# The opening of an attention and experts kernel, ordered anew for each engine

## The chip, the cores and the metric

The kernel runs on one core of a Trainium2 chip. The metric is the device time of one execution in microseconds (us); the median of several executions is what two kernels are compared by. Five engines work side by side, each through its own queue in order: TensorE (PE, with its weight loads as PEld), VectorE (DVE), ScalarE (ACT), GpSimd (POOL), and SyncE (SP), which here issues nearly all DMAs. TensorE's clock has two levels in the records, 2.4 GHz (granted clock 1.0) and 1.2 GHz (0.5).

## The reference, cut to what matters

```
scores = q @ k.T / 8, causal; a = softmax(scores); local = a @ v        # B=2, H=8, S=576, D=64
phi(x) = where(x > 0, x, exp(x) - 1) + 1
mem_out = (phi(q) @ M_prev) / (phi(q) . z_prev + 1e-6)
attn = g * mem_out + (1 - g) * local,  g = sigmoid(beta)                  # per head
x = attn as [1152 tokens, 512]
x = relu(x @ w_in)**2 @ w_out                                             # 512 -> 2048 -> 512
out = sum over 4 experts of p_e * (relu(x @ w1_e) @ w2_e)                 # 512 -> 1024 -> 512
```

## The kernel before, in words

The 1152 tokens are nine tiles of 128 (`TILES`), in three chunks: chunk 0 is tiles 7 and 8 (the first 128 positions of both batches), chunk 1 is tiles 0 to 3, chunk 2 is tiles 4 to 6. The first feed-forward layer, `ffn1`, runs once for each chunk; while it runs for one chunk, the attention of the next is woven in (`mix`), so TensorE always has matmuls of a feed-forward layer to put between those of attention. Only for chunk 0 is there no layer to hide behind: its attention is the **opening**, and TensorE's dense work begins with the first `hpa` matmul of `mm_in` (L101), which needs the finished tokens `first_x` (tile `y`, written at L222).

In the opening chunk 0 has four units: (tile 7, heads 0 to 3), (8, 0 to 3), (7, 4 to 7), (8, 4 to 7), which are called u0, u1, u2, u3 below. A unit goes through score matmuls (L303, into a bank of PSUM), four masked row maxima on VectorE (`top`, L189, and the bias `nb`, L314), four exps on ScalarE (L320), a transpose on TensorE (L332) copied back by VectorE (L335), and the value matmuls (L352). Beside it the feature maps `phi(q)` are made in two halves (exp L181, VectorE L183 and L184), `mem` multiplies them by the memory `mzd` in three groups of heads (L365, copied by ScalarE, L368), and `combine` scales and adds the two parts for each tile (`zeroth` L199 to L204, `first` L211 and L212, `second` L218 to L222).

The order of the opening is a string of step names, `order`, carried out step by step inside `tc.manual_schedule()`, where every engine keeps the written order. Outside that block only TensorE keeps the written order; for the other engines a planner with its own idea of durations decides, and it may put an instruction that it takes to be ready into an earlier gap of its engine, the opening's gaps too. `tc.keep_in_program_order(x)` forbids that for one instruction: x stays behind what was written before it on its engine.

Three more pieces of work meet here. `convert` (the steps `c` and `f`) turns the 64-bit weight words of `ffn1` into floats, one half block at a time: a DMA of 512 KB (L647), two ScalarE passes (L657, L660), two VectorE passes (L661, L664), and a write of 256 KB to DRAM (L667); there are 32 half blocks, the layer eats them in order, and four buffers hold words that are on their way. `value_scale` takes ten sums of squares of `v` on ScalarE (L405), wanted only in chunk 2. `c1` is the attention of chunk 1: its first two pairs of units are scored in the opening (`S0`, `S1`), the others, its feature maps and the squares are written later, in `rest`.

Of the kernel before, what the change touches and what calls it, by code (L numbers as in the profile page):

```python
# [10 lines left out]
F32 = mybir.dt.float32  # L11
# [5 lines left out]
AF = mybir.ActivationFunctionType  # L17
# [4 lines left out]
P = 128  # L22
# [30 lines left out]
def attention_then_experts(ctx, tc, qa, ka, va, qc, kc, vc, mz, beta, w1, probs, w2, out):  # L53
# [122 lines left out]
        nc.vector.tensor_scalar(out=gate1, in0=gate, scalar1=-1.0, scalar2=1.0, op0=ALU.mult, op1=ALU.add)  # L176
        yield

    def phi(out, e, q):

        nc.scalar.activation(out=e, in_=q, func=AF.Exp)  # L181
        yield
        nc.vector.tensor_scalar_min(e, e, 1.0)  # L183
        nc.vector.scalar_tensor_tensor(out=out, in0=q, scalar=1.0, in1=e, op0=ALU.add, op1=ALU.max)  # L184
        yield
# [7 lines left out]
    def combine(t, pool, xl, xm, sm, guard, pv, ps, eng, nm=1, gate1=gate1):  # L193


        cf = pool.tile([P, 2, H], F32, tag="cf", name="cf", bufs=2)

        def zeroth():
            nc.vector.tensor_scalar_add(cf[:, 0], sm, guard)  # L199
            nc.vector.tensor_scalar_add(cf[:, 1], xm[:, :, D], 1e-6)  # L200
            nc.vector.reciprocal(out=cf, in_=cf)
            nc.vector.tensor_mul(cf[:, 0], cf[:, 0], gate1)
            nc.vector.tensor_mul(cf[:, 1], cf[:, 1], gate)
            nc.gpsimd.tensor_mul(xm[:, :, 0:D], xm[:, :, 0:D], cf[:, 1, :, None].to_broadcast([P, H, D]))  # L204

        def first():
            if not pv:
                eng.tensor_mul(xl, xl, cf[:, 0, :, None].to_broadcast([P, H, D]))
            for hs, part in pv() if pv else ():
                n = hs.stop - hs.start  # L210
                nc.vector.tensor_mul(xl[:, hs], part, cf[:, 0, hs, None].to_broadcast([P, n, D]))  # L211
            eng.tensor_add(xl, xl, xm[:, :, 0:D])  # L212

        def second():
            tp = ps.tile([P, NK, P], F32, tag="m", name="tp", bufs=nm)
            xf = xl.rearrange("p h d -> p (h d)")
# [14 lines left out]

    def opening(c0, c1, first_layer):

        sc, ph, low, gt = [c0.scores(p) for p in c0.pairs], c0.phis(0), [], gates()
        later = [c1.scores(p) for p in c1.pairs[:2]]
        units = [u for p in c0.pairs for u in p]
        xs = []
        third = (slice(0, 3), slice(3, 6), slice(6, 8))
        steps = dict(
            g=lambda: next(gt), c=lambda: next(cv), f=lambda: next(cv), w=lambda: next(first_layer), l=lambda: c1.load(1),  # L240
            x=lambda: xs.extend(c0.combine(t) for t in range(*CHUNKS[0])),
            a0=lambda: xs[0][0](), a1=lambda: xs[0][1](), a2=lambda: low.append(xs[0][2]()), a3=lambda: low[0](),
            b0=lambda: xs[1][0](), b1=lambda: xs[1][1](), b2=lambda: low.append(xs[1][2]()), b3=lambda: low[1](),
        )
        for i in range(2):
            steps[f"s{i}"] = lambda i=i: next(sc[i])
            steps[f"v{i}"] = lambda i=i: [c0.values(u) for u in c0.pairs[i]]
            steps[f"S{i}"] = lambda i=i: next(later[i])
            steps[f"p{i}"] = lambda i=i: next(ph[i])
        for i in range(4):  # L250
            steps[f"t{i}"] = lambda i=i: c0.turn(units[i], nc.vector)
        for i in range(3):
            steps[f"m{i}"] = lambda i=i: c0.mem(0, third[i])
        order = (
            "s0 p0 g s0 g s0 s1 s0 p1 s0 s1 l f s1 t0 p0 x s1 t1 S0 s1 p1 m0 v0 t2 S0 m1 t3 "
            "m2 v1 S0 c S0 a0 b0 S1 S0 a1 S1 b1 c S1 a2 b2 w S1 c b3 a3 S1 c"
        )
        for k in order.split():
            steps[k]()

    def attention_a(c, pool, eng, banks):
# [9 lines left out]
        def load(r):  # L271
            raw = pool.tile([P, H, P], F32, tag="qa", name="qa", bufs=2)
            ka_t[r] = kva.tile([P, H, P], F32, name=f"ka{r}")
            for hs in (slice(0, 4), slice(4, 8)):
                nc.sync.dma_start(out=ka_t[r][:, hs], in_=ka[r, :, hs])
                nc.sync.dma_start(out=raw[:, hs], in_=qa[r, :, hs])
            q[r] = [raw, None, pool.tile([P, B, H, D + 1], F32, tag="xm", name="xm", bufs=2)]
            load_v(r)

        def load_v(r):  # L280
            for b in range(B):
# [2 lines left out]

        def phis(r):
            e = q[r][1] = pool.tile([P, H, P], F32, tag="phia", name="phia", bufs=2)
            return [phi(e[:, hs], e[:, hs], q[r][0][:, hs]) for hs in (slice(0, 4), slice(4, 8))]

        def s_(pair):
            scs = {}  # L290
            for u in pair:
# [3 lines left out]
                scs[u] = banks[0].tile([P, 512], F32, tag="s", name="sc", bufs=banks[1])  # L295
# [74 lines left out]
        def combine_(t):  # L370
# [13 lines left out]
            )  # L384

        return SimpleNamespace(
            pairs=pairs, load=load, phis=phis, scores=s_, turn=t_, values=v_, mem=mem, combine=combine_,
        )

    def value_scale(pool, banks):  # L390

        todo = [(b, k) for k in (3, 4) for b in range(B)]
        vsq = pool.tile([P, 3 * B + len(todo)], F32, tag="vsq", name="vsq", bufs=1)

        def stage(b, k):
            x = pool.tile([P, 4, P], F32, tag="vstage", name="vstage", bufs=2)
            nc.sync.dma_start(out=x, in_=vc[b, :, :, k].rearrange("j p d -> p j d"))
            return x.rearrange("p j d -> p (j d)")

        parts = [va_t[b, r].rearrange("p h d -> p (h d)") for r in range(3) for b in range(B)]  # L400
        for i in range(vsq.shape[1]):
            if i < len(todo):
                parts.append(stage(*todo[i]))
            sq = pool.tile([P, 512], BF16, tag="sq", name="sq", bufs=2)
            nc.scalar.activation(out=sq, in_=parts[i], func=AF.Square, accum_out=vsq[:, i:i + 1])  # L405
            yield
        total = banks[0].tile([P, vsq.shape[1]], F32, tag="m", name="total", bufs=banks[2])
        nc.tensor.matmul(total, lhsT=ones, rhs=vsq, start=True, stop=True)
        nc.vector.tensor_reduce(out=vs, in_=total, axis=AX.X, op=ALU.add)
        power(vs, vi, 77)  # L410
        nc.vector.tensor_mul(gate1v, gate1, vi[:, 0:1].to_broadcast([P, H]))
        yield

    def rest(x, scale):
# [7 lines left out]
        for i, pair in enumerate(x.pairs):  # L422
            t, kn, h0, nh = pair[0]
            r = TILES[t][0][1] // P
            if i >= 2:
                plan(i - 2, 0, lambda p=pair: run(x.scores(p)))
            for u in pair:
                plan(i, 2, lambda u=u: x.turn(u))
# [5 lines left out]
            if h0 + nh == H:  # L434
                for n, u in enumerate(pair):
# [4 lines left out]
                        parts[0]()  # L440

                    plan(i, 5 + n, make)
                    plan(i, 7 + n, lambda parts=parts: parts[1]())
# [8 lines left out]
    def attention_b(pool, ps):  # L452
# [158 lines left out]
        for i in range(len(units) + lag + 3):  # L611
# [9 lines left out]
            if 0 <= i - lag < len(units):  # L621
                t, j = units[i - lag]
                m = [values(t, j)[0]] + m
                if j == 3:
                    xl, xm, mx, nb, sm = st[t]
                    fs = combine(t, pool, xl, xm, sm, 1e-9 * 2.0**14, None, ps, nc.gpsimd, gate1=gate1v)
                    m = m + [lambda fs=fs: (fs[0](), fs[1]())]
# [10 lines left out]
    def convert(pool):  # L638
# [10 lines left out]
        for i in range(3):  # L649
            fetch(i)  # L650
        yield
        for i, (f, half) in enumerate(todo):
            fetch(i + 3)
# [94 lines left out]
    with ExitStack() as ca:  # L748
# [5 lines left out]
        with tc.tile_pool(name="ps_0", bufs=1, space=PSUM) as ps_0:  # L754
            with tc.manual_schedule():
# [372 lines left out]
```

## Time before, and what the profile says of it

| | before |
|---|---|
| median of 3 runs | 743.21 us (741.28 to 744.14) |
| the profiled execution | 740.5 us, of which the span from first to last instruction is 738.7 us |
| TensorE busy | 686.9 us, 93% of the span |
| VectorE, ScalarE, GpSimd busy | 549.1, 430.2, 241.4 us |
| TensorE busy from 36 us to 136 us | 90.4 of 100 us |
| first matmul of the feed-forward layer | 35.48 us after the span's start |

All instants are counted from the start of the span. Before 35.48 us TensorE has only the small matmuls of the opening; after it, it is busy nine tenths of the time or more to the end.

### The profile page before, as it was taken

The numbers are of one execution on the slowest core, as the hardware profiler recorded it, in microseconds if no ns is written. First come the engines' busy times: TensorE is split into PE (matmuls) and PEld (weight loads), VectorE is DVE, ScalarE is ACT, GpSimd is POOL, SyncE is SP. The second block draws the span as 40 slices with busy tenths as digits, with TensorE's granted clock in tenths as the row PEclk, the third lists the DMA queues.
The fourth block names the chain that finished last, engine by engine and source line by source line (L and its number), as shares of the span: only waits on it lengthen the run. The fifth ranks groups of instructions, "written<-read, shape, count | busy, mean of one in ns | idle before, by whom it ended". The sixth has DMA issues, their size and how long they took to land.

```text
span 738.7 us, 12576 instructions
## 1 busy us (share of the span) xinstructions
PE 686.9 (93%) x4604; PEld 487.1 (66%) x4604; DVE 549.1 (74%) x1057; ACT 430.2 (58%) x844; POOL 241.4 (33%) x249
## 2 busy tenths in 40 slices
PE   6588899989899998999999989999999999999997
PEld 4466777767677787989865655566655555555553
DVE  4867858479989874746879968989787685867763
ACT  5687767376665534887776756655535353535341
POOL 1101101253533237645623433344432323141400
PEclk7799999999999999999999999999999999999999
DMA  9788765177885543685412323233342222100002
GB/s 286 229 297 289 254 219 180 58 262 222 196 197 122 122 114 83 238 302 169 131 59 93 108 85 115 87 113 94 109 168 75 100 81 91 58 1 1 1 1 71
DMA packets 65422, 101.25 MB, mean 137 GB/s; under 512 B 32656, under 2 KB 34704, under 8 KB 65360
## 3 DMA queue, kind: packets, MB, share of 16 engines
q1 hardware_dynamic: 65216, 100.45, 44.5%
q8 instruction: 36, 0.59, 0.3%
q14 instruction: 26, 0.21, 0.1%
q10 hardware_dynamic: 144, 0.00, 0.0%
HBM read 82.87 MB, written 10.75 MB: 127 GB/s over the span
## 4 chain that ended last, share of the span: by engine, by line
PE 52%; DVE 18%; ACT 11%; DMA 9%; issue 6%; POOL 3%; SPq 0%; DVEq 0%; ACTq 0%; POOLq 0%
PE o L1016 19%; PE pe L924 16%; DMA raw<-in_w 4%; PE y L723 3%; PE hpb L106 3%; PE pv L584 2%; DMA wraw<-w1s 2%; DVE bits L661 2%; PE y L721 2%; POOL w L84 2%; PE hpa L101 2%; DVE g L713 1%; ACT a L320 1%; DVE a L189 1%; PE sc L516 1%
## 5 line engine op out<-in xcount | busy, mean ns | idle before, releaser
L1016 PE MATMUL o<-w,g 128*128 128x512 f16 x864 | 218.5, 379 | 7.0 <-DVE g L940 3.8
L924 PE MATMUL pe<-xs,wu 128*128 128x256 f16 (+1 forms) x1344 | 196.5, 286 | 2.1 <-DVE h L945 2.0
L924 PEld LDWEIGHTS <-wu 128*128 128x128 f16 x1344 | 131.0, 98 | 70.3 <-issue 3.8
L1016 PEld LDWEIGHTS <-g 128*128 128x128 f16 x864 | 83.7, 98 | 77.8 <-DVE g L940 7.1
L84 POOL TENSOR_TENSOR w<-wraw,w 128x512 fp32r<-128x512 f32 x49 | 73.1, 1498 | 104.6 <-ACT w L83 104.3
L939 ACT ACTIVATE g<-h 128x512 f16<-128x512 f32 (+1 forms) x64 | 43.3, 677 | 105.7 <-DVE h L945 105.7
L723 PE MATMUL y<-g,w 128*128 128x512 f32 (+1 forms) x384 | 90.7, 372 | 1.5 <-ACT w L83 0.7
L954 POOL TENSOR_TENSOR u<-u,p 128x256 f32<-128x256 f32 (+1 forms) x32 | 32.3, 1011 | 132.7 <-ACT p L953 110.9
L723 PEld LDWEIGHTS y<-g,w 128*128 128x128 f32 x384 | 68.2, 189 | 9.7 <-ACT w L83 1.0
L940 DVE SCALAR_TENSOR_TENSOR g<-h,g 128x512 f16<-128x512 f32 (+1 forms) x64 | 50.4, 788 | 26.3 <-ACT g L939 26.0
L106 PE MATMUL hpb<-x,w 128*128 128x512 f32 x192 | 53.2, 414 | 4.7 <-DVE r L707 4.6
L945 DVE SCALAR_TENSOR_TENSOR h<-pe,u 128x256 f32<-128x256 f32 (+1 forms) x96 | 42.8, 451 | 19.8 <-PE pe L924 15.7
L891 POOL TENSOR_TENSOR ws<-raw 128x256 f32<-128x256 f32 x32 | 23.3, 727 | 101.9 <-issue 88.7
L888 DVE SCALAR_TENSOR_TENSOR wu<-ws,wpow,wu 128x512 f16<-128x512 f32 x64 | 50.9, 835 | 2.9 <-ACT wu L899 2.9
L833 DVE SCALAR_TENSOR_TENSOR w<-raw,wpow,w 128x512 f16<-128x512 f32 x64 | 48.0, 755 | 0.7 <-ACT w L832 0.6
L83 ACT ACTIVATE w<-wraw 128x512 fp32r<-128x512 f32 x64 | 39.5, 623 | 13.0 <-DMA wraw<-w1s 6.6
L106 PEld LDWEIGHTS hpb<-x,w 128*128 128x128 f32 x192 | 36.3, 196 | 13.6 <-DVE r L707 6.4
L832 ACT ACTIVATE w<-raw,wpow 128x512 f16<-128x512 f32 x64 | 44.6, 709 | 0.9 <-PE o L1016 0.9
L829 ACT ACTIVATE junk<-raw 128x1024 bf16<-128x1024 f32 x32 | 33.5, 1048 | 19.0 <-DMA raw<-in_w 18.9
L189 DVE CUSTOM_DVE_ANT_0 a<-sc,mask 128x384 f32<-128x384 f32 (+4 forms) x80 | 35.9, 477 | 11.1 <-PE sc L303 5.5
L204 POOL TENSOR_TENSOR xm<-xm,cf 128x512 f32<-128x512 f32 x9 | 10.6, 1184 | 102.1 <-ACT at L337 42.7
L106 PE MATMUL hpc<-x,w 128*128 128x384 f32 x192 | 37.3, 339 | 3.1 <-POOL w L84 2.0
(159 smaller groups left out, 1200.0 us busy)
## 6 DMA issues: line engine op xcount, KB each, us to landing
raw<-in_w SPq DMA_DIRECT2D x64, 512.0 KB, 3.4
w<-in_w SPq DMA_DIRECT2D x32, 512.0 KB, 4.4
wraw<-w1s SPq DMA_DIRECT2D x64, 256.0 KB, 3.1
w1s<-bits SPq DMA_DIRECT2D x32, 256.0 KB, 2.5
kraw<-in_kc SPq DMA_DIRECT2D x8, 576.0 KB, 4.1
vraw<-in_vc SPq DMA_DIRECT2D x8, 320.0 KB, 3.7
qraw<-in_qc SPq DMA_DIRECT2D x4, 512.0 KB, 4.9
out<-acc SPq DMA_DIRECT2D x8, 256.0 KB, 2.1
```

The lines of the kernel that those rows point to most:

```text
L84: eng.tensor_sub(w[:, 1], raw, w[:, 0].bitcast(F32))
L106: nc.tensor.matmul(acc, lhsT=w[:, a, kk * P:(kk + 1) * P], rhs=xs_r[c][:, b, kk, :], start=(i == 0), stop=(i == 3 * NK - 1),)
L189: nc.vector.tensor_tensor_reduce(out=dst, in0=sc, in1=msk, op0=ALU.add, op1=ALU.max, scale=1.0, scalar=-3.0e38, accum_out=m)
L723: nc.tensor.matmul(yacc[d], lhsT=w[:, a, d * P:(d + 1) * P], rhs=g[:, b], start=(first and i == 0), stop=(last and i == 2),)
L832: nc.scalar.activation(out=w0, in_=x, func=AF.Copy, scale=s)
L833: nc.vector.scalar_tensor_tensor(out=w1, in0=x, scalar=s, in1=w0, op0=ALU.mult, op1=ALU.subtract)
L888: nc.vector.scalar_tensor_tensor(out=w[:, 1, ks], in0=x, scalar=s1, in1=w[:, 0, ks], op0=ALU.mult, op1=ALU.subtract)
L924: nc.tensor.matmul(acc, lhsT=w[:, wa, k, kk * P:kk * P + P], rhs=x[:, xb, kk], start=(m == 0), stop=(m == 5))
L939: nc.scalar.activation(out=g[:, 0], in_=hm, func=AF.Relu)
L940: nc.vector.scalar_tensor_tensor(out=g[:, 1], in0=hm, scalar=0.0, in1=g[:, 0], op0=ALU.max, op1=ALU.subtract)
L945: nc.vector.scalar_tensor_tensor(out=out, in0=acc, scalar=HID, in1=x, op0=ALU.mult, op1=ALU.add)
L1016: nc.tensor.matmul(outs[t], lhsT=g[:, gb, r:r + P], rhs=w[:, wa], start=(p == 0 and m == 1 and k == 0), stop=(p == 3 and m == 0 and k == 2),)
```

## The change

`order` is written anew. The weight words are fetched, and chunk 1's second block of q, k and v is loaded, at its start; `v` of the first block is loaded behind the memory `mzd`. The scores of the second pair (u2, u3) go into the two banks that the values use later (tag `pv`), so that four score units stand at once. The steps go unit by unit of one tile (u0, u2, then u1, u3), so that tile 7 is combined while tile 8 is still in its exps. `combine`'s `first` gives its add back as a step of its own (`y0`, `y1`). In the opening only one pair of chunk 1 is scored instead of two (the second is the first step of `rest`), and two half blocks are converted instead of five; the first of them is cut into its ScalarE and its VectorE half. The squares of `v` and the feature maps of chunk 1 are pinned by `keep_in_program_order`, which puts them behind the opening, and the staged loads of `v` for the squares are written three squares ahead of their use.

```
-    def phi(out, e, q):
-        nc.scalar.activation(out=e, in_=q, func=AF.Exp)
+    def phi(out, e, q, hold=lambda x: x):
+        hold(nc.scalar.activation(out=e, in_=q, func=AF.Exp))
...
-            eng.tensor_add(xl, xl, xm[:, :, 0:D])
+            return lambda: eng.tensor_add(xl, xl, xm[:, :, 0:D])
...
-        sc, ph, low, gt = [c0.scores(p) for p in c0.pairs], c0.phis(0), [], gates()
-        later = [c1.scores(p) for p in c1.pairs[:2]]
+        sc = [c0.scores(p, spot) for p, spot in zip(c0.pairs, (("s", 3), ("pv", 2)))]
+        ph, gt, later = c0.phis(0), gates(), c1.scores(c1.pairs[0])
...
+            steps[f"z{i}"] = lambda i=i: (xs.update({i: c0.combine(CHUNKS[0][0] + i)}), xs[i][0]())
+            steps[f"x{i}"] = lambda i=i: adds.update({i: xs[i][1]()})
+            steps[f"y{i}"] = lambda i=i: adds[i]()
+            steps[f"o{i}"] = lambda i=i: xs[i][2]()
...
         order = (
-            "s0 p0 g s0 g s0 s1 s0 p1 s0 s1 l f s1 t0 p0 x s1 t1 S0 s1 p1 m0 v0 t2 S0 m1 t3 "
-            "m2 v1 S0 c S0 a0 b0 S1 S0 a1 S1 b1 c S1 a2 b2 w S1 c b3 a3 S1 c"
+            "c l c s0 p0 p0 g g p1 s1 s0 s0 s0 s1 s1 p1 m0 t0 s1 t2 v0 s0 m1 m2 t1 v2 z0 x0 S s1 z1 t3 c "
+            "y0 v1 v3 o0 x1 y1 o1 c S S w S S S"
         )
...
+        hold = [tc.keep_in_program_order] * (c > 0)
+        return [phi(e[:, hs], e[:, hs], q[r][0][:, hs], *hold) for hs in (slice(0, 4), slice(4, 8))]
...
-            if i < len(todo):
-                parts.append(stage(*todo[i]))
+            if i in (3, 4, 7, 8):
+                parts.append(stage(*todo[len(parts) - 6]))
...
-            nc.scalar.activation(out=sq, in_=parts[i], func=AF.Square, accum_out=vsq[:, i:i + 1])
+            tc.keep_in_program_order(
+                nc.scalar.activation(out=sq, in_=parts[i], func=AF.Square, accum_out=vsq[:, i:i + 1])
+            )
...
-            if i >= 2:
+            if i:
                 plan(i - 2, 0, lambda p=pair: run(x.scores(p)))
...
-        for i in range(3):
-            fetch(i)
+        fetch(0)
+        yield
+        fetch(1)
+        fetch(2)
         yield
...
+            if i == 0:
+                yield
...
+                c0.load_v(0)
                 opening(c0, c1, layer)
```

## Rows read from the trace of the kernel before

**Rows 1.** The page's busy time of each engine, with its share of the span.
```profile
PE 686.9 (93%) x4604; PEld 487.1 (66%) x4604; DVE 549.1 (74%) x1057; ACT 430.2 (58%) x844; POOL 241.4 (33%) x249
```
**Rows 2.** Windows: stretch, PE, PEld, DVE, ACT, POOL busy, granted clock, DMA share, GB/s.
```profile
10.00:20.00 10.00, 7.32 (x30) 5.10 (x30) 6.03 (x25) 9.61 (x42) 0.00 (x0) 0.50 1.05 361
...
30.00:40.00 10.00, 6.69 (x29) 4.94 (x30) 7.86 (x22) 7.13 (x21) 0.06 (x1) 0.52 0.81 258
35.50:55.50 20.00, 16.99 (x120) 13.30 (x121) 14.05 (x34) 17.76 (x45) 0.00 (x0) 0.87 0.88 299
36.00:136.00 100.00, 90.39 (x772) 70.46 (x770) 69.89 (x179) 74.34 (x174) 9.63 (x7) 0.96 0.72 240
```
**Rows 3.** The chain that ended last, 0 to 45 us: start, length, what.
```profile
3.08 7.49 DMA va<-in_va
...
10.59 0.72 ACT sq L405 x2
11.31 1.54 ACT a L320 x8
12.85 0.52 ACT phia L181
...
16.61 2.07 PE sc L303 x14
...
24.32 0.58 ACT mag L657
...
26.89 0.08 DVE cf L199
...
30.75 1.10 PE tp L218 x4
...
33.71 1.10 PE tp L218 x4
...
35.48 2.93 PE hpa L101 x6
```
**Rows 4.** Timeline of ScalarE: start, length, what, idle time before it and its releaser.
```profile
9.48 0.63 ACT L405 ACTIVATE sq<-va 128x512 bf16<-128x512 f32 x1 [4.06 <-DMA va<-in_va]
```
**Rows 5.** Timeline of VectorE: the bias of the first unit.
```profile
7.74 0.17 DVE L314 TENSOR_SCALAR nb<-mx 128x4 f32<-128x4 f32 x1
```
**Rows 6.** Timeline of TensorE: memory products, scores of a pair at either clock.
```profile
18.61 1.66 PE L365 MATMUL pm<-mzd,phia 128*128 128x130 f32 x6
...
24.91 1.16 PE L303 MATMUL sc<-ka,qa 64*128 64x128 f32 x16
...
38.34 2.08 PE L303 MATMUL sc<-ka,qa 64*128 64x128 f32 x16
```
**Rows 7.** Groups of VectorE's instructions by shape, 0 to 36 us.
```profile
L184 DVE SCALAR_TENSOR_TENSOR phia<-qa,phia 128x512 f32<-128x512 f32 x6 | 3.9, 681 | 0.0
...
L189 DVE CUSTOM_DVE_ANT_0 a<-sc,mask 128x256 f32<-128x256 f32 x8 | 3.0, 414 | 0.0
...
L183 DVE TENSOR_SCALAR phia<-phia 128x512 f32<-128x512 f32 x6 | 2.5, 418 | 3.9 <-ACT phia L181 3.9
...
L212 DVE TENSOR_TENSOR xl<-xl,xm 128x512 f32<-128x512 f32 x2 | 1.6, 787 | 0.1
L211 DVE TENSOR_TENSOR xl<-pv,cf 128x256 f32<-128x256 f32 x4 | 1.5, 409 | 0.0
L661 DVE SCALAR_TENSOR_TENSOR bits<-mag,bits 128x512 int32<-128x512 int32 x2 | 1.4, 684 | 0.4 <-ACT bits L660 0.4
```
**Rows 8.** Timeline of SyncE: when the DMAs of memory and words are issued.
```profile
3.55 1.42 SPq L772 DMA_DIRECT2D mzd<-in_mz  x2
...
11.23 2.23 SPq L647 DMA_DIRECT2D w<-in_w  x4
```
**Rows 9.** DMA issues of 3.5 to 4.4 us and of 12.9 us: size, us to landing.
```profile
mzd<-in_mz SPq DMA_DIRECT2D x2, 130.0 KB, 7.6
...
w<-in_w SPq DMA_DIRECT2D x1, 512.0 KB, 10.0
```

More of the change, by code (lines that the diff above doesn't have):

```diff
@@ L232, in opening @@
     def opening(c0, c1, first_layer):
-        sc, ph, low, gt = [c0.scores(p) for p in c0.pairs], c0.phis(0), [], gates()
-        later = [c1.scores(p) for p in c1.pairs[:2]]
+        sc = [c0.scores(p, spot) for p, spot in zip(c0.pairs, (("s", 3), ("pv", 2)))]
+        ph, gt, later = c0.phis(0), gates(), c1.scores(c1.pairs[0])
         units = [u for p in c0.pairs for u in p]
-        xs = []
-        third = (slice(0, 3), slice(3, 6), slice(6, 8))
+        xs, adds = {}, {}
         steps = dict(
[L240 to L243, printed above, removed]
+            g=lambda: next(gt), c=lambda: next(cv), w=lambda: next(first_layer), l=lambda: c1.load(1), S=lambda: next(later, None),
@@ L244, in opening @@
         )
         for i in range(2):
-            steps[f"s{i}"] = lambda i=i: next(sc[i])
-            steps[f"v{i}"] = lambda i=i: [c0.values(u) for u in c0.pairs[i]]
-            steps[f"S{i}"] = lambda i=i: next(later[i])
+            steps[f"s{i}"] = lambda i=i: next(sc[i], None)
             steps[f"p{i}"] = lambda i=i: next(ph[i])
-        for i in range(4):
-            steps[f"t{i}"] = lambda i=i: c0.turn(units[i], nc.vector)
-        for i in range(3):
-            steps[f"m{i}"] = lambda i=i: c0.mem(0, third[i])
+            steps[f"z{i}"] = lambda i=i: (xs.update({i: c0.combine(CHUNKS[0][0] + i)}), xs[i][0]())
@@ L254, in opening @@
+            steps[f"x{i}"] = lambda i=i: adds.update({i: xs[i][1]()})
+            steps[f"y{i}"] = lambda i=i: adds[i]()
+            steps[f"o{i}"] = lambda i=i: xs[i][2]()
+        for i, u in enumerate(units):
+            steps[f"t{i}"] = lambda u=u: c0.turn(u, nc.vector)
+            steps[f"v{i}"] = lambda u=u: c0.values(u)
+        for i, hs in enumerate((slice(0, 3), slice(3, 6), slice(6, 8))):
+            steps[f"m{i}"] = lambda hs=hs: c0.mem(0, hs)
         order = (
-            "s0 p0 g s0 g s0 s1 s0 p1 s0 s1 l f s1 t0 p0 x s1 t1 S0 s1 p1 m0 v0 t2 S0 m1 t3 "
@@ L277, in load @@
             q[r] = [raw, None, pool.tile([P, B, H, D + 1], F32, tag="xm", name="xm", bufs=2)]
-            load_v(r)
+            if r:
+                load_v(r)
         def load_v(r):
@@ L286, in phis, with s_ @@
             e = q[r][1] = pool.tile([P, H, P], F32, tag="phia", name="phia", bufs=2)
-            return [phi(e[:, hs], e[:, hs], q[r][0][:, hs]) for hs in (slice(0, 4), slice(4, 8))]
-        def s_(pair):
+            hold = [tc.keep_in_program_order] * (c > 0)
+            return [phi(e[:, hs], e[:, hs], q[r][0][:, hs], *hold) for hs in (slice(0, 4), slice(4, 8))]
+        def s_(pair, spot=None):
             scs = {}
+            tag, bufs = spot or ("s", banks[1])
             for u in pair:
@@ L294, in s_ @@
                     st[t] = [pool.tile([P, H], F32, tag=x, name=x, bufs=4) for x in ("mx", "nb", "sm")]
-                scs[u] = banks[0].tile([P, 512], F32, tag="s", name="sc", bufs=banks[1])
+                scs[u] = banks[0].tile([P, 512], F32, tag=tag, name="sc", bufs=bufs)
                 a_[u] = pool.tile([P, 512], F32, tag="a", name="a", bufs=3 + 4)
@@ L386, in attention_a @@
         return SimpleNamespace(
-            pairs=pairs, load=load, phis=phis, scores=s_, turn=t_, values=v_, mem=mem, combine=combine_,
+            pairs=pairs, load=load, load_v=load_v, phis=phis, scores=s_, turn=t_, values=v_, mem=mem, combine=combine_,
         )
@@ L442, in rest @@
                     plan(i, 5 + n, make)
-                    plan(i, 7 + n, lambda parts=parts: parts[1]())
+                    plan(i, 7 + n, lambda parts=parts: parts[1]()())
                     plan(i + 1, 1.5 + n, lambda parts=parts: parts[2]()())
@@ L626, in attention_b @@
                     fs = combine(t, pool, xl, xm, sm, 1e-9 * 2.0**14, None, ps, nc.gpsimd, gate1=gate1v)
-                    m = m + [lambda fs=fs: (fs[0](), fs[1]())]
+                    m = m + [lambda fs=fs: (fs[0](), fs[1]()())]
                     late[i + 1] = [lambda fs=fs: fs[2]()()]
@@ L647, in fetch @@
                 nc.sync.dma_start(out=words[i].rearrange("p n t -> p (n t)"), in_=w1[f, half].bitcast(I32))
-        for i in range(3):
-            fetch(i)
+        fetch(0)
+        yield
+        fetch(1)
+        fetch(2)
         yield
```

## The prediction

> **What bounds the kernel now.** I read the page first: TensorE is busy 93% of the span and no other engine comes near it [rows 1]. The windows then say where the rest is lost: from 36 us to 136 us, the layer of chunk 0 with chunk 1's attention, TensorE works 90.4 of 100 us, while in the opening it has little to do and does part of it at the half clock, 0.50 from 10 to 20 us and 0.52 from 30 to 40 us [rows 2]. So the opening is a stretch bound by waits, and what follows is nearly all bound by TensorE; an earlier first `hpa` (35.48 us [rows 3]) is worth its own length as long as the work pushed behind it finds room there.
>
> The chain of waits says what the opening's length consists of. It starts with 7.49 us for the DMA of `va`, goes on with two squares on ScalarE, and only then come the exps of the first unit, at 11.31 us [rows 3]. The squares are written far later, in `rest`; the planner has put them in front. ScalarE stood 4.06 us before the first of them [rows 4], while the bias that the exps want was finished at 7.74 + 0.17 = 7.9 us [rows 5]. Further down the same chain runs through a feature map between the exps, the scores of chunk 1, a conversion in front of `combine` (24.32 to 26.89 us), and 2.96 us between the starts of the two tiles' transposes (30.75, 33.71) [rows 3]. None of these is needed for `first_x`, or not there.
>
> **The change, what it takes out of that chain.**
> - Squares pinned behind the opening: the first exps start at 7.9 instead of 11.31 us [rows 3, 5], 3.4 us.
> - Feature-map exps moved in front of the exps: two of 0.52 us [rows 3] (one of the two is shown), 1.0 us. They are hidden by VectorE's row maxima, which run until 7.9 us.
> - Scores of chunk 1 no longer in front of the memory products: 2.07 us [rows 3], at the half clock.
> - Conversion no longer in front of `combine`: 26.89 - 24.32 = 2.6 us [rows 3]. Its ScalarE half now lies behind the last exps, under the value matmuls, and its VectorE half behind the last add.
> - The two tiles' last steps together: between the transposes VectorE needs only two multiplies and an add, 2 x 0.41 + 0.79 = 1.6 us [rows 7], of the 2.96 us, so 1.4 us.
>
> Together 10.5 us: 35.5 would become 25.0 us.
>
> **What it adds there.** On ScalarE the copy of the first memory products now stands in front of the exps of u2, and waits for `mzd`. In the trace its two DMAs are issued one after the other from 3.55 us, and take 7.6 us to land [rows 8, 9], so until about 11.9 us; there they were first wanted at 18.61 us [rows 6], so nobody waited. The exps of u0 end at 7.9 + 1.5 = 9.4 us. Bounds: no wait, or memory at 11.9 us and the products at half clock, 1.66 us [rows 6], which is 13.6, or 4.2 us late. The change issues the 512 KB of `va` behind `mzd`, so I put the landing at 9.5 us, with the products 11.2 us: 1.8 us late. The pair of chunk 1 still scored in the opening stands in front of the last transpose: 1.16 us at full clock [rows 6], so 1.2 us. The rest of the regrouping (four score banks, `y0` as a step of its own) I cost at nothing: the second pair's scores wait for q and k, not for a bank, and the add waits for GpSimd's product behind VectorE's own copies. If a bank wait came back, it would be one row-maximum of a unit, about 1 us.
>
> The first `hpa` then starts at 25.0 + 1.8 + 1.2 = 28.0 us, 7.5 us earlier.
>
> The Trainium skill ("DMA: Bandwidth & Descriptors", Specifications) says that transfers below 512 bytes do not reach the line rate; `mzd` is moved in runs of 65 floats, 260 bytes, so by that page it would land as late whatever stands behind it. The trace agrees so far that 130 KB took 7.6 us [rows 9]; it is rival three below.
>
> **What is pushed behind the opening.** TensorE: 16 score instructions of the second pair, 1.16 us at full and 2.08 us at half clock [rows 6]; between the ends, since the clock after the sparse end of the opening was 0.52 [rows 2], I take 1.6 us. VectorE: the maxima of two pairs of chunk 1, 4 units x 2 heads x 0.41 = 3.3 us, two halves of feature maps at 0.42 + 0.68 = 2.2 us, one conversion 2 x 0.68 = 1.4 us [rows 7], 6.9 us that were done before 35.5 us and now are not. From 35.5 to 55.5 us VectorE has 20 - 14.05 = 5.95 us idle [rows 2]. Bounds: all hidden, or 6.9 us on the path. I take what does not fit, 1.0 us. ScalarE is fuller (17.76 of 20 us [rows 2]); it receives exps, feature maps and a conversion, but gives up its squares there, and its excess overlaps VectorE's. The squares, pinned, go to where ScalarE is idle a quarter of the time (74.3 of 100 us [rows 2]). The staged loads, three squares ahead of use, cost nothing while a step of the weave lasts longer than a landing of a few us; else a square is late, and with it only chunk 2's scale.
>
> **The sum.** 7.5 - 1.6 - 1.0 = 4.9 us. The profiled execution took 740.5 us and would take 735.6. The median of the runs lies 2.7 us above that execution, so 743.2 - 4.9 = 738.3 us is the prediction, with a range of its own of 736 to 740 us. Half a per cent, 3.7 us or 739.5 us, is about what a measurement of this kernel can tell from no change.
>
> **The rivals.**
> 1. All hidden: the opening is denser on TensorE, its clock comes back earlier, and the backlog vanishes in idle time. Memory without a wait (1.8), no VectorE rest (1.0), and 1.5 us of the half-rate work regained make 4.9 + 4.3 = 9.2: 734.0 us. For it: in 10 to 20 us the clock was half while TensorE was busy 7.32 us [rows 2], so there is something to regain. Against: TensorE still pauses for exps.
> 2. A conversion takes the place of the squares (slower). The conversions of `rest` are not pinned. If the planner puts the byte pass (L660) of the third half block into a gap before the exps of u1 or u3, ScalarE stands until those words land; before, words issued from 11.23 us on took up to 10.0 us, until 22.9 us [rows 8, 9]. Exps due at about 13 us would then start at 22.9, 9.9 us late: 743.2 - 4.9 + 9.9 = 748.2 us. It makes the kernel slower from a stand of 4.9 us on. For it: the squares did exactly this [rows 4]. Against: the words are asked for earlier now, so they may have landed by then.
> 3. Memory as late as before, at 11.9 us: 4.2 instead of 1.8 us, gain 2.5: 740.7 us.
> 4. VectorE's 6.9 us all on the path, because its queue has the conversions in front of the row maxima that TensorE waits for: 743.2 - 4.9 + 5.9 = 744.2 us. For it: ScalarE, which feeds it, has only 2.24 us idle there. Against: the idle 5.95 us of its own [rows 2].
> 5. The change does not do what it says, because the words' DMA paces the first layer and an earlier start only waits earlier: 743 us. For it: DMA share 0.88 from 35.5 to 55.5 us; against: 0.72 over the hundred us [rows 2].
>
> **How the numbers follow.** Chances: forecast 0.42, rivals one to five 0.17, 0.10, 0.12, 0.11, 0.08. Faster by over half a per cent (under 739.5): four fifths of the forecast 0.34, rival one 0.17, a sixth of rival three 0.02, in all 0.53. Slower (over 746.9): rival two 0.10 and the tail of rival four 0.01, in all 0.11. Within: the rest, 0.36. The range leaves out rival two and the lower half of rival one: 733.5 to 744.5 us.
>
> **What would show it.** Right: no square and no feature map of chunk 1 before the first `hpa`; the first exps at about 8 us; first `hpa` between 26 and 30 us; the busy share of TensorE in the hundred us after it still near 90%. Step by step: the wait of ScalarE's copy for the memory products (1.8 us, or 4); VectorE's maxima as the releaser of TensorE in the first 20 us after the opening (1.0 us or more). The prediction is wrong if ScalarE waits for a DMA of words inside the opening, if the first `hpa` moves by 7 us and the layer's end by less than 3, or if the clock stays at one level through 10 to 40 us.

## The result, and the profile after

The changed kernel takes 732.29 us (median of 4 runs, 728.97 to 732.89) against 742.53 us before (4 runs): a ratio of 0.9857, 95% interval 0.9823 to 0.989. That is 10.2 us less; forecast were 4.9 us, and the time lies below the range. The profiled execution takes 731.94 us with a span of 730.1 us, 8.6 us less than the one before.

The page's busy times [rows 1] are nearly unchanged but for TensorE, 4.7 us less with the same 4604 matmuls:

```profile
PE 682.2 (93%) x4604; PEld 483.6 (66%) x4604; DVE 549.3 (75%) x1057; ACT 430.2 (59%) x844; POOL 241.9 (33%) x249
```

The chain that ended last, from 0 to 26 us, beside [rows 3]:

```profile
1.19 3.59 DMA qa<-in_qa
...
7.76 0.20 DVE a L189
...
10.29 0.89 ACT a L324 x4
...
11.20 0.43 DVE phia L183
...
13.00 1.12 PE pv L356 x16
14.12 2.47 PE pm L369 x10
...
17.48 0.69 DVE at L339
...
21.30 1.15 DVE xl L212
...
23.22 0.70 DVE xl L212
23.92 0.04 issue
23.97 0.67 PE tp L218 x4
...
25.39 2.90 PE hpa L101 x6
```

The 7.49 us for `va`, the squares, the scores of chunk 1 and the conversion are gone from it. The first `hpa` starts at 25.39 us, 10.1 us earlier. The first squares stand at 60.05 us, and no ScalarE wait for words lies in the opening. The timelines of ScalarE and TensorE at the steps that the prediction put a time to:

```profile
8.22 0.40 ACT L324 ACTIVATE a<-a,nb 128x128 f32<-128x128 f32 x1 [0.95 <-DVE nb L318]
...
9.77 0.47 ACT L372 ACTIVATE xm<-pm 128x390 f32<-128x390 f32 x1
...
8.18 0.91 PE L369 MATMUL pm<-mzd,phia 128*128 128x130 f32 x6 [0.27 <-DVE nb L318]
...
18.36 1.16 PE L307 MATMUL sc<-ka,qa 64*128 64x128 f32 x16
...
25.39 2.90 PE L101 MATMUL hpa<-y,bits 128*128 128x256 f32 x6 [0.77 <-ACT y L222]
28.21 1.27 PE L307 MATMUL sc<-ka,qa 64*128 64x128 f32 x16
```

The two transfers of `mzd` are now issued at 2.6 and 3.4 us, ahead of `va`, and land 4.6 us later instead of 7.6 [rows 9]; of the view of the tile up to 9 us:

```profile
L782 SPq DMA_DIRECT2D mzd<-in_mz x2: 625/687/749, 2.6 to 3.4; - x2
...
DMA to landing us min/median/max: 4.6/4.6/4.7
```

So the second lands at about 8.0 us, and the memory products start at 8.18. The releaser that the timeline names for them, VectorE's `nb` (the bias), is nothing that they read, and the feature map was done at 6.6 us, so their wait of 0.27 us was for `mzd`. But nobody waits for the products: they end at 9.1 us, and ScalarE copies them at 9.77, right behind the exps of u0.

What became of the 10.1 us is read from the stretch of the first layer, from the first `hpa` to the first matmul of the next layer, `hpb` (L106). The windows of after, in the columns of [rows 2], the last line this stretch:

```profile
10.00:20.00 10.00, 8.78 (x71) 6.93 (x71) 5.89 (x25) 6.98 (x29) 0.93 (x1) 0.66 1.05 356
30.00:40.00 10.00, 6.37 (x41) 4.68 (x39) 9.06 (x30) 9.49 (x28) 0.00 (x0) 1.00 0.92 291
35.50:55.50 20.00, 17.12 (x163) 13.84 (x163) 16.68 (x49) 17.74 (x44) 2.08 (x2) 1.00 0.95 336
25.39:138.43 113.04, 100.00 (x850) 79.27 (x851) 82.15 (x214) 87.06 (x210) 12.09 (x9) 0.99 0.68 229
```

and the same stretch of before, which the rows ahead of the prediction don't show:

```profile
35.48:147.51 112.03, 101.49 (x834) 80.02 (x835) 75.38 (x188) 78.12 (x182) 12.09 (x9) 0.96 0.65 218
```

It is 1.0 us longer. TensorE has 16 matmuls more in it (the second pair's scores, 1.16 us at full clock [rows 6]) and is idle 13.0 instead of 10.5 us; yet it is busy 1.5 us less, because the granted clock is 0.99 instead of 0.96. So 9.1 of the 10.1 us are left at `hpb`, and 8.6 at the end. The waits of TensorE from 24 to 132 us, with total, number and longest, say where it is idle; the second fence is the line for row maxima in the same window of before:

```profile
PE atp L336 <- DVE mx L189: 5.0, 6, 1.8
PE pv L356 <- ACT at L341: 1.9, 3, 1.4
PE pm L369 <- DVE phia L184: 1.6, 1, 1.6
PE sc L307 <- DVE mx L189: 1.4, 1, 1.4
```

```profile
PE atp L332 <- DVE mx L189: 4.1, 5, 2.0
```

It waits for VectorE's row maxima, 6.4 us in all instead of 4.1, and once for chunk 1's feature map. VectorE's timeline there shows conversions (L671, L674) standing between the maxima of chunk 1:

```profile
30.88 0.42 DVE L189 CUSTOM_DVE_ANT_0 a<-sc,mask 128x256 f32<-128x256 f32 x1
...
31.22 0.69 DVE L674 SCALAR_TENSOR_TENSOR bits<-w,bits 128x512 int32<-128x512 int32 x1
31.83 0.42 DVE L189 CUSTOM_DVE_ANT_0 a<-sc,mask 128x256 f32<-128x256 f32 x1
...
32.57 1.38 DVE L671 SCALAR_TENSOR_TENSOR bits<-mag,bits 128x512 int32<-128x512 int32 x2
33.87 1.29 DVE L674 SCALAR_TENSOR_TENSOR bits<-w,bits 128x512 int32<-128x512 int32 x2
35.07 0.42 DVE L189 CUSTOM_DVE_ANT_0 a<-sc,mask 128x256 f32<-128x256 f32 x1
```

### The profile page after: what moved, and what is told of

Its sections match the earlier page's. It is cut to its first block, busy times and chain, and to the rows that moved or that the text cites. A ratio compares the mean times of both kernels' runs of the same rounds, so it can differ in the third digit from the quotient of the medians.

```text
span 730.1 us, 12567 instructions
## 1 busy us (share of the span) xinstructions
PE 682.2 (93%) x4604; PEld 483.6 (66%) x4604; DVE 549.3 (75%) x1057; ACT 430.2 (59%) x844; POOL 241.9 (33%) x249
## 4 chain that ended last, share of the span: by engine, by line
PE 53%; DVE 19%; ACT 12%; DMA 8%; issue 5%; POOL 3%; SPq 0%; DVEq 0%; ACTq 0%; POOLq 0%
PE o L1027 19%; PE pe L935 16%; PE y L733 4%; DMA raw<-in_w 3%; PE hpb L106 3%; DMA wraw<-w1s 2%; PE hpa L101 2%; PE pv L590 2%; PE y L731 2%; DVE a L189 2%; DVE wu L899 2%; ACT a L324 2%; DVE g L723 1%; PE hpc L106 1%; POOL w L84 1%
## 5 line engine op out<-in xcount | busy, mean ns | idle before, releaser
L106 PE MATMUL hpb<-x,w 128*128 128x512 f32 x192 | 53.3, 415 | 4.8 <-DVE r L717 4.7
L106 PEld LDWEIGHTS hpb<-x,w 128*128 128x128 f32 x192 | 36.1, 196 | 13.9 <-DVE r L717 7.0
L106 PE MATMUL hpc<-x,w 128*128 128x384 f32 x192 | 37.6, 340 | 4.4 <-POOL w L84 2.5
L899 DVE SCALAR_TENSOR_TENSOR wu<-raw,wpow,wu 128x768 f16<-128x768 f32 x32 | 33.4, 1042 | 7.0 <-ACT wu L904 6.4
```

The lines of the kernel that those rows point to most:

```text
L106: nc.tensor.matmul(acc, lhsT=w[:, a, kk * P:(kk + 1) * P], rhs=xs_r[c][:, b, kk, :], start=(i == 0), stop=(i == 3 * NK - 1),)
L899: nc.vector.scalar_tensor_tensor(out=w[:, 1, ks], in0=x, scalar=s1, in1=w[:, 0, ks], op0=ALU.mult, op1=ALU.subtract)
```

## The experiments

Each changes one thing of the kernel before ("old") or of the changed one ("new"), or builds on the order of 11. The ratio is to the kernel before on the same chip, whose median was 741.05 to 742.53 us, so a difference of two experiments under about 2 us, or with overlapping intervals, is not told; the last four columns are of the one profiled execution: first `hpa`, length of the first layer's stretch, TensorE's busy time in it, granted clock in it.

| | median us (runs) | ratio, 95% interval | `hpa` | stretch | busy | clock |
|---|---|---|---|---|---|---|
| old | 742.53 (4) | | 35.5 | 112.0 | 101.5 | 0.96 |
| new | 732.29 (4) | 0.9857, 0.9823 to 0.989 | 25.4 | 113.0 | 100.0 | 0.99 |
| 1 old, both pins | 743.33 (9) | 1.0032, 1.0013 to 1.0051 | 29.8 | 120.2 | 105.1 | 0.92 |
| 2 old, squares pinned | 740.86 (10) | 0.9986, 0.9957 to 1.0014 | 34.7 | 114.1 | 100.7 | 0.97 |
| 3 new, no pins | 732.36 (4) | 0.9887, 0.9871 to 0.9904 | 28.9 | 110.4 | 100.5 | 0.98 |
| 4 new, `v` first | 737.82 (10) | 0.995, 0.9925 to 0.9974 | 27.2 | 113.5 | 101.6 | 0.97 |
| 5 new, conversion in front | 734.1 (4) | 0.9911, 0.9881 to 0.9941 | 26.7 | 113.7 | 102.4 | 0.97 |
| 6 new, three banks | 731.67 (4) | 0.9852, 0.9804 to 0.9899 | 24.3 | 114.6 | 101.7 | 0.97 |
| 7 new, scores in front | 732.05 (4) | 0.9874, 0.9846 to 0.9902 | 24.8 | 114.9 | 102.3 | 0.97 |
| 8 new, two pairs | 738.16 (10) | 0.9959, 0.9928 to 0.999 | 27.6 | 116.5 | 102.7 | 0.94 |
| 9 old, one pair | 744.43 (9) | 1.0043, 1.0023 to 1.0064 | 32.6 | 116.0 | 104.4 | 0.94 |
| 10 new, maps in opening | 737.48 (10) | 0.9939, 0.9918 to 0.996 | 25.5 | 119.8 | 106.9 | 0.92 |
| 11 new, maxima first | 729.17 (4) | 0.9811, 0.9761 to 0.986 | 23.9 | 112.6 | 101.7 | 0.97 |
| 12 = 11 and 10 | 734.53 (4) | 0.9911, 0.9886 to 0.9936 | 25.3 | 115.8 | 100.9 | 0.99 |
| 13 = 11, maps free | 729.34 (4) | 0.984, 0.982 to 0.9861 | 26.6 | 112.5 | 102.6 | 0.96 |
| 14 new, waits filled | 731.34 (4) | 0.9883, 0.9838 to 0.9927 | 24.5 | 116.6 | 103.3 | 0.96 |
| 15 old, waits filled | 740.55 (10) | 0.9992, 0.9974 to 1.001 | 35.1 | 110.4 | 99.1 | 0.98 |
| 16 = 11 and 14 | 727.48 (4) | 0.9823, 0.979 to 0.9856 | 22.9 | 111.7 | 101.5 | 0.97 |
| 17 new, five buffers | 734.06 (4) | 0.9913, 0.9882 to 0.9943 | 25.5 | 114.7 | 102.5 | 0.96 |
| 18 = 16 and 17 | 732.51 (4) | 0.9898, 0.9861 to 0.9935 | 23.5 | 112.6 | 102.1 | 0.97 |

**1. The two pins in the old order.**

```
+            hold = [tc.keep_in_program_order] * (c > 0)
+            tc.keep_in_program_order(
                 nc.scalar.activation(out=sq, in_=parts[i], func=AF.Square, accum_out=vsq[:, i:i + 1])
```

> The kernel before with nothing but the two pins (squares, feature maps of chunk 1). Theory: the pins are worth what the squares held up, 3.4 us at the first exps (11.3 to about 7.9 us), and a little between the two last transposes; the rest of the opening's 10.1 us came from the order. First hpa at 31 to 32 us, time 738.5 to 740 us against 742.5. Rival: the pins are nearly the whole change, and the order only shuffles: first hpa at 27 us or earlier, time 733 to 735 us.

The first `hpa` is 5.7 us earlier, and the median is 2.3 us above that of the kernel before. The stretch behind it is 8.2 us longer, with TensorE busy 3.6 us more at a clock of 0.92: the pinned feature maps of chunk 1 now stand behind all exps written before them and come out at 42.56 us, too late. The waits of TensorE from 30 to 132 us have this line:

```profile
PE pm L366 <- DVE phia L184: 4.1, 1, 4.1
```

**2. The squares' pin alone, in the old order.** The second half of that edit.

> The kernel before with the squares pinned and the feature maps of chunk 1 free. In the run with both pins the first hpa came 5.7 us earlier and the layer ended 2.5 us later: the memory products of chunk 1 waited 4.1 us for the pinned feature maps. Theory: that wait is what ate the gain; with the maps free the squares' 3 to 4 us come through: first hpa at 31 to 32 us, no wait of that kind over 2 us, 738 to 740 us against 741. Rival: in the old order the weave is bound by its own chain, and an earlier first hpa is lost there whatever is pinned: 741 to 744 us.

The first exps do start 3.1 us earlier (at 8.09 instead of 11.22 us on ScalarE's timeline), but ScalarE's timeline shows what was behind the squares: a feature map of chunk 1, hoisted by the planner between the exps of chunk 0.

```profile
8.09 0.40 ACT L320 ACTIVATE a<-a,nb 128x128 f32<-128x128 f32 x1 [2.22 <-DVE nb L314]
...
13.48 0.63 ACT L181 ACTIVATE phia<-qa 128x512 f32<-128x512 f32 x1 [1.68 <-DMA qa<-in_qa]
```

That load lands where it did, so the wait moves there. Of the 3.1 us 0.8 reach the first `hpa`, and none the median that can be told.

**3. The new order without pins.** Both edits of 1 undone in the new kernel.

> The changed kernel without its two pins. Theory: the squares stand before the first exps again, but v lands at about 9 us now, so the exps start near 10 us instead of 8.2; feature maps of chunk 1 between the exps add 1 to 2 us: first hpa 28 to 30 us, time 735 to 737 us against 732. Rival (pins are the whole): back to 35 us and 742 us.

The first `hpa` is 3.5 us later (squares in front of the exps again, which start at 10.90 us), the stretch 2.6 us shorter (maps early, no wait for `phia`), the median the same. The pins move work between opening and layer, and neither order gains by them.

**4. `v` ahead of the memory again.**

```
-            if r:
-                load_v(r)
+            load_v(r)
...
-                c0.load_v(0)
```

> The changed kernel with v of the first block loaded ahead of the memory again. It measures the term that the prediction took at 1.8 us and that the run showed as none. Theory: the memory lands only because it is in front of v; behind 512 KB it lands near 10 us or later, the first memory products start 2 us or more after 8.2 us, ScalarE's copy holds the exps of u2, first hpa 27 to 29 us, time 734 to 736 us. Rival: the memory would have been in time anyway: products at 8.2 to 9 us, first hpa at 25.4 to 26 us, time 732 us.

`mzd` takes 8.1 us to land; this is the line among the DMA issues of the first 9 us, and below it ScalarE's copy of the first products:

```profile
mzd<-in_mz SPq DMA_DIRECT2D x2, 130.0 KB, 8.1
```

```profile
14.49 0.50 ACT L371 ACTIVATE xm<-pm 128x390 f32<-128x390 f32 x1 [3.78 <-PE pm L368]
```

The memory products start at 12.81 instead of 8.18 us, and the exps of u2 stand behind a wait of 3.78 us. The first `hpa` is 1.8 us later, the median 5.5 us up. The profiled execution, 732.79 us, was the fastest run of this version and lies only 0.9 us above that of the changed kernel, so where the rest of the 5.5 us lies isn't shown. The wait of the prediction's third rival is real; the new kernel avoids it by loading `mzd` first. The edit also delays the second half of q, which u2 and u3 need: it lands 6.4 instead of 4.5 us after its issue.

**5, 6, 7. Three terms of the opening.** The first conversion whole ahead of `combine`; all four units' scores in the three banks of tag `s`; the first scores of chunk 1 ahead of two groups of memory products.

```
5  "... t1 v2 c c z0 x0 S s1 z1 t3 "  "y0 v1 v3 o0 x1 y1 o1 S S w S S S"
6  zip(c0.pairs, (("s", 3), ("s", 3)))
7  "... t2 v0 s0 S m1 m2 t1 v2 z0 x0 s1 z1 t3 c "
```

> The changed kernel with the first conversion whole and in front of the combination of tile 7 again, as the old order had it. Theory: it stands on the chain with about 2.6 us there: first hpa near 28 us, and nothing is given back later, so 734 to 735 us. Rival: the two VectorE passes fit beside the value matmuls, and ScalarE's passes are done early: first hpa at 25.5 to 26.5 us, time 732 to 733 us.

> The changed kernel with the second pair's scores of chunk 0 in the three score banks again, not in those of the values. Theory: the second pair's matmuls then wait for the maxima of u0 and u1 (VectorE, until about 9 us) instead of starting at 6.75 us; VectorE has work of its own until then, so under 1 us on the first hpa: 25.4 to 26.5 us, time 732 to 733 us. Rival: the transposes need the same banks too, and tile 7's chain waits again: first hpa at 28 us or later, 735 us.

> The new kernel with the first eight score matmuls of chunk 1 ahead of the second and third group of memory products again, as they stood before. By the prediction's term (2.07 us at half clock for 14 of them) this costs about 1.2 us on first `hpa`, 26.6 instead of 25.4, and as much on the median, 733.5 us. Rival (TensorE waits for ScalarE's exps there anyway): first `hpa` within 0.4 us of 25.4, the median within 1 us of 732.3.

Only the conversion costs: 1.3 us at the first `hpa`. Its median is 1.8 us up, or 4.0 by the ratios (0.0054 of 742), with intervals that just overlap, so the median alone does not tell it. Banks and place of the scores cost nothing that can be told; both first `hpa` are even 0.6 to 1.1 us earlier.

**8. The second pair of chunk 1 back in the new opening.**

```
+        more = c1.scores(c1.pairs[1])
+            T=lambda: next(more, None),
-            "y0 v1 v3 o0 x1 y1 o1 c S S w S S S"
+            "y0 v1 v3 o0 x1 y1 T o1 c S S T T w S S T T S"
```

> The changed kernel with chunk 1's second pair scored in the opening again (its matmuls in front of tile 8's last transposes, its maxima and exps in the opening's tail). Theory: what was pushed behind the opening costs little there (1.0 us given back in the whole weave), so undoing it brings nothing: first hpa at 26 to 27 us, time 731 to 734 us. Rival: having only one pair in front is what lets the weave run: 736 us or more.

The first `hpa` is 2.2 us later, the stretch 3.5 us longer, the median 5.9 us up. ScalarE, with the exps of two pairs and the pinned maps behind them, is the bound for ten microseconds. The window from 30 to 40 us:

```profile
30.00:40.00 10.00, 6.46 (x40) 4.82 (x38) 6.41 (x20) 10.00 (x31) 0.00 (x0) 0.84 0.62 190
```

TensorE's longest wait from 27 to 60 us is for the map that ScalarE brings late:

```profile
PE pm L371 <- DVE phia L184: 3.1, 1, 3.1
```

**9. The other side of 8: one pair in the old opening.**

```
-        later = [c1.scores(p) for p in c1.pairs[:2]]
+        later = [c1.scores(c1.pairs[0])] * 2
-            "m2 v1 S0 c S0 a0 b0 S1 S0 a1 S1 b1 c S1 a2 b2 w S1 c b3 a3 S1 c"
+            "m2 v1 S0 c S0 a0 b0 S0 a1 b1 c a2 b2 w c b3 a3 c"
```

> The old order, old banks, nothing pinned; only the second pair of chunk 1 leaves the opening and becomes the first step of `rest`. Theory (what counts is how much work stands in front of first `hpa` on TensorE and behind it on ScalarE and VectorE; putting the pair back into the new order cost 6 us): first `hpa` one to two us earlier than 35.5, and 3 to 6 us off the median, 736 to 739 us. Rival (the pair matters only in the new order, because the old one ends its opening on the squares and conversions anyway): first `hpa` within 1 us of 35.5 and the median within 2 us of before.

My theory, that the pair's place was the gain, falls: the first `hpa` is 2.9 us earlier, but the stretch 4.0 us longer, at a clock of 0.94, and the kernel is slower. The pair's place pays only together with the rest of the order.

**10, 11, 12. Feature maps as steps of the opening; row maxima ahead of maps and gates.**

```
10   "y0 v1 v3 o0 x1 y1 o1 c S S w S S S q Q0 Q1 Q0 Q1"    (q, Q0, Q1: chunk 1's maps)
11   "c l c s0 p0 g p1 s1 s0 p0 s1 s0 s0 m0 t0 s1 s1 p1 g t2 v0 s0 m1 m2 t1 v2 z0 x0 S s1 z1 t3 c "
```

> The new kernel with the feature maps of chunk 1's first block as written steps at the tail of the opening, so that their VectorE part stands ahead of the weave's. Theory (the 1.6 us that TensorE waits for `phia` in the new kernel is on the path): 1 to 2 us less, 730.5 to 731.5 us, and that wait gone. Rival (moved in front of the weave's row maxima they delay those instead, as the second pair did): 733 us or more, with the wait moved to `sc` or `atp`.

> The changed kernel with the steps that follow unit by unit on VectorE too: the maxima of u0 first (in front of the feature map and the gates), those of u2 in front of u1, the copy of u0's transpose in front of u3's maxima. Theory: first exps at 7.2 instead of 8.2 us, value matmuls of u0 at about 11 instead of 13 us, first hpa at 24 us or a little earlier, time 730 to 732 us. Rival: the half-rate TensorE from 11 to 18 us sets the pace there, and first hpa stays at 25 us: 732 us.

> The order with each unit's row maxima ahead of the feature maps and gates (729.2 us alone) and the feature maps of chunk 1 as steps of the opening. Theory: both gains add, 727.5 to 728.5 us. Rival: the wait for `phia` is cover for another, and the time is that of the order alone, 729 us or more.

In 10 the rival holds. The wait for `phia` is gone, and in its place stands a longer one, since the maps' VectorE part now stands between the maxima, from 31.05 to 34.02 us; TensorE's waits from 24 to 60 us:

```profile
PE sc L309 <- DVE mx L189: 3.3, 1, 3.3
```

The order of 11 has a median 3.1 us below that of the changed kernel, with overlapping intervals: the first `hpa` is 1.5 us earlier at no cost behind it. With the maps in front as well (12) that is lost again, beyond the intervals.

**13. Order 11 with the maps free.** `hold = []`, squares still pinned.

> The order with the row maxima ahead of maps and gates (729.2 us), squares pinned as in the new kernel, the feature maps of chunk 1 not pinned. Theory (in the new order the pin of the squares is worth the 3.5 us of first `hpa` that the kernel without pins lost, and the pin of the maps costs the 1.6 us wait for `phia`): first `hpa` near 24, no such wait, 727.5 to 728.5 us. Rival (free maps are hoisted into the opening's gaps, ahead of exps or maxima, as in the kernel before): first `hpa` a microsecond or more later and 729 us or more.

As without pins, the maps go back into the opening (first `hpa` 2.8 us later) and the median stays.

**14, 15, 16. TensorE's waits filled.** Idle matmuls of zeros into the bank of the warm-up.

```
+  F=lambda: nc.tensor.matmul(warm, lhsT=wt[:, 0:P], rhs=wt, start=True, stop=True)
14, 16  "y0 v1 F F v3 F o0 x1 F F F y1 o1 c S S w S S S F F F"
15      "... S1 F(14 times) a2 F(6 times) b2 w S1 c b3 a3 S1 c F F"
```

> The new kernel with nine idle matmuls (zeros into the bank of the warm-up, 128x512 bf16, nothing reads them) put into the waits of TensorE from 20 to 25 us: two ahead of the second tile's values, one and three ahead of its two transposes, three ahead of the first `hpa`. Theory (the waits there let the clock fall, and the first feed-forward matmuls pay): the granted clock from 25 to 28.4 us is 1.0 instead of 0.5, the first six `hpa` take 1.5 instead of 2.9 us, first `hpa` within 0.3 us of 25.4, and the median 1 to 2 us less, 730.5 to 731 us. Rival (what the clock is granted there does not hang on those waits): the six `hpa` still take 2.9 us, the fillers only delay them, 732.5 us or more.

> The kernel before with 22 of the same idle matmuls in the waits of its opening, 14 in the 4.7 us ahead of the first tile's transposes, six in the 1.9 us between the two, two ahead of the first `hpa`. Theory (about 4 of the 10 us of the new kernel are clock, of 3.3 us for each 0.01 of the mean granted clock over all runs so far, 0.975 before and 0.988 after): the half clock from 30.4 to 40.6 us is gone, first `hpa` stays at 35.5, and 2 to 4 us come off the median, 738 to 740 us. Rival: the clock falls later instead, and the median stays within 1 us of before.

> The same order with the pins of the new kernel and the nine idle matmuls of the first experiment of this group. Theory: its half clock from 25 to 35 us (six `hpa` in 2.4 us, the scores of a unit pair in 1.9) goes, 1.5 to 3 us less than 729.2, 726 to 727.7 us. Rival: no change or later, 729 us or more.

TensorE's timeline of 14:

```profile
23.52 0.81 PE L239 MATMUL warm<-wt 128*128 128x512 bf16 x3
24.45 1.53 PE L101 MATMUL hpa<-y,bits 128*128 128x256 f32 x6
...
28.18 0.46 PE L307 MATMUL sc<-ka,qa 64*128 64x128 f32 x2
30.74 1.84 PE L307 MATMUL sc<-ka,qa 64*128 64x128 f32 x14 [2.10 <-DVE mx L189]
32.51 2.46 PE L101 MATMUL hpa<-y,bits 128*128 128x256 f32 x6
```

The first six `hpa` take 1.5 instead of 2.9 us. That the waits had let the clock fall is likely and not shown: in all four versions with idle matmuls the six take 1.5 to 1.6 us, but so they do in three of the sixteen executions without (4, 6 and 12), right behind a wait as long as that of the changed kernel. This is TensorE's timeline of 6:

```profile
24.32 1.53 PE L101 MATMUL hpa<-y,bits 128*128 128x256 f32 x6 [0.76 <-ACT y L222]
```

In 14 TensorE then arrives earlier at the maxima, waits 2.1 instead of 1.4 us for them, and now the next matmuls run at the half clock. The medians are 1.0 us (14) and 1.7 us (16) lower, the ratios a little higher: no difference that can be told. In 15 the half clock between 30 and 40 us [rows 2] is gone, as this window shows,

```profile
30.00:40.00 10.00, 7.89 (x51) 5.56 (x52) 9.86 (x30) 7.75 (x22) 0.12 (x1) 1.00 0.81 257
```

and the median does not move by what can be told. Version 16, 727.48 us, has the lowest median of all and beats the kernel before beyond doubt; against 11 and the changed kernel the intervals overlap.

**17, 18. Fewer buffers for converted words,** so that conversions run less far ahead.

```
-            bits = pool.tile([P, DM], I32, tag="bits", name="bits", bufs=8)
+            bits = pool.tile([P, DM], I32, tag="bits", name="bits", bufs=5)
```

> The new kernel with five instead of eight buffers for converted words, so that the planner's conversions can run less far ahead of the layer that eats them. In the new kernel VectorE makes four conversions, 1.3 us each, between 30 and 38 us, among the row maxima for which TensorE waits 1.4 us at 32.4 and 1.0 us at 36.0. Theory (what was pushed behind the opening stands behind conversions that are not due yet): fewer conversions there, these two waits shorter, the layer's stretch 1 to 3 us shorter, 729 to 731 us. Rival (the planner places them by its own times, and the layer needs them soon after): the same waits, or TensorE waiting for `bits`, 732 us or more.

> The fastest order so far (row maxima first, idle matmuls in the waits, 727.5 us) with the same five buffers. Theory: 1 to 3 us less, 724.5 to 726.5 us. Rival: no change or later, 727.5 us or more.

Both are slower by the medians, by 1.8 and 5.0 us (the second beyond the intervals), and the waits for maxima stay (4.7 and 1.4 us in 17). Fewer buffers did not take the conversions from between the maxima.

## Why the prediction was wrong, step by step

Right in kind, too small by half: the opening shortened by more than the sum, and less was given back. The miss is 10.2 - 4.9 = 5.3 us: 2.6 at the first `hpa` (10.1 instead of 7.5), 1.1 behind it (1.5 given back instead of 2.6), and 1.6 of luck, because the profiled executions differ by 8.6 us and the medians by 10.2. The steps that failed are the two terms added to the opening, 3.0 us that both came to nothing on the path, and a backlog priced without the clock.

- **What bounds it.** In the changed kernel an earlier first `hpa` was worth its length but for 1.5 us. That is no rule: in 1 and 9 it came 5.7 and 2.9 us earlier and the kernel was slower, in 3 and 13 it came 3.5 and 2.8 us later at no cost. It hangs on the prediction's own condition, that the work pushed behind finds room.
- **Removed, 10.5 us.** The size came out, 10.1 us at the first `hpa`, but not term by term. *Squares, 3.4 us*: the exps start 3.0 us earlier (8.22 against 11.22 on the two timelines), yet the pin that does it is worth nothing on the median by itself (2, 3). As a price of the pin the term named no next late thing behind the squares: the q of chunk 1, for a map that the planner had hoisted. *Feature maps, 1.0 us*: misread; the chain of before holds a map of chunk 1, not of chunk 0 alone, and what the pin of the maps costs behind the opening (4.1 us in 1, 1.6 in the new kernel) was not in the sum. *Scores before the memory products, 2.07 us*: worth nothing (7). *Conversion, 2.6 us*: 1.3 (5). *Two tiles' last steps*: the transposes start 1.46 us apart (22.51 and 23.97), 1.6 were forecast. So the terms overlapped, and no one of them alone stands for the whole.
- **Added, 3.0 us.** Both terms failed. *Pair of chunk 1, 1.2 us*: its matmuls take 1.16 us at full clock, as forecast, but they run at 18.36 us while the chain goes through VectorE, from 17.48 to 23.92 us, so they cost nothing. *Memory, 1.8 us*: mis-sized; 0 in the changed kernel. The step that failed took the landing at 9.5 us and the products at half clock, 1.66 us. The first issue moved from 3.55 to 2.60 us as well as past `va`, the second transfer landed at about 8.0 (3.4 + 4.6), and the products took 0.91 us, so that they were done at 9.1 us, ahead of the end of u0's exps at 9.77. Experiment 4 gives the mechanism its price: 1.8 us at the first `hpa` when `va` goes first. The same move brought the second half of q earlier, which no term has: the scores of u2 and u3 start at 6.75 instead of 8.43 us. The Trainium skill ("DMA: Bandwidth & Descriptors", Specifications) has transfers below 512 bytes short of line rate. The runs of `mzd` stayed at 260 bytes, while its landing took 4.6, 7.6 or 8.1 us. That it would land as late whatever stands behind it does not follow from the page, and it did not happen: here the place in the queue made the difference. *Four banks at nothing*: right (6).
- **Pushed behind, 2.6 us.** It was 1.0 us by `hpb`. TensorE's share was 1.16 us, not 1.6, as the clock was full. VectorE's was not 1.0 but 2.5 us of idle TensorE. What the sum left out is the clock: busy time fell by 1.5 us in spite of 1.16 us more work, so 2.7 us came back with a clock of 0.99 instead of 0.96. That is one execution of each: 6 and 7, no slower, had 101.7 and 102.3 us busy at 0.97, a longer stretch and an earlier first `hpa`, so the split is sure to no better than about 2 us. The sign of the pair's term was wrong too in the new order: left in front, it cost 5.9 us (8).
- **The sum.** 10.1 - 1.0 - 0.5 (behind `hpb`) = 8.6 us in the profiled execution, against 7.5 - 2.6. The medians differ by 10.2; the profiled execution of before lay 2.0 us below its median of 4 runs, that of after 0.35. By the profiled executions alone it would have been 743.2 - 8.6 = 734.6 us, inside the range.
- **The rivals.** The first came about, by its own first and third terms (no memory wait on ScalarE, work regained by the clock in the executions profiled), though it kept VectorE's rest at nothing, and there it was wrong. The second and fifth did not come; the third is avoided, as 4 shows; the fourth has the right releaser, but 2.5 us of idle TensorE and not 6.9.
- **What would show it.** No square or map of chunk 1 ahead of the first `hpa`, exps at 8.2 us, the maxima as releaser: as written. ScalarE's copy did not wait for the memory products. The first `hpa` was below its 26 to 30 us, for the two terms that cost nothing; TensorE's share stayed at 100.0 of 113.0.

**What is settled and what is open.** Shown: neither pins nor banks make the gain; loading the memory first and one pair instead of two each cost time when undone in the new order, 5.5 and 5.9 us by the medians; one pair alone in the old order costs time. The later conversion is worth 1.3 us at the first `hpa`; its 1.8 us on the median is not told. From the first `hpb` to the end of the span all twenty executions take 589 to 595 us, while `hpb` starts between 134.7 and 150.0 us: what the versions gain or lose lies mostly ahead of it, in opening and stretch together. The parts don't add up; that TensorE's idle time and its clock answer to each other is a guess at the reason. Open is how much of the 10.2 us is clock. Over the 191 runs with a clock on record a run's distance from its kernel's mean goes with its mean granted clock, 3.5 us for each 0.01, and the two kernels' means are 0.9745 and 0.9877, so about 4.6 us would go with it. But in 15 the mean rose to 0.981 by filling alone and the median stayed: the clock is at least in part a trace of the waits and not a cause of its own.

## What to carry to other kernels

When a stall is taken out of an engine's queue, look up what is due next on that engine, a planner's hoisted instructions included: here 0.8 of 3.1 us were left behind the next load. Undo each part in the new order, not only in the old one, since a part may be worth 6 us there and less than nothing alone. A small load that heads a chain goes ahead of the large one that nobody waits for yet. Filling TensorE's waits brought nothing here that can be told: in 14 it arrived earlier and waited longer for the next maxima.

## What was not expected of the hardware

The granted clock differs between runs of one and the same kernel, and the time with it: experiment 4 took 732.8 us at a mean of 0.985 and 740.5 at 0.972. With matmuls of zeros in waits of 0.4 to 0.8 us the clock behind the opening was 1.0 in four executions of four, where it is 0.5 in the changed kernel's, but it was 1.0 without them too in three executions with waits as long (4, 6 and 12). In 14 the half clock came back at 30.7 us, behind a wait of 2.1 us.
